# An SSM convolution with gated FFN, forward and backward: the kernel factors are generated over 128x16 positions, kept in DRAM and DMA-transposed for the parameter gradients

## The chip, the cores and the metric

One core of a Trainium2 chip runs the whole program. The metric is the device time of one execution in microseconds. Beside the times there is one execution taken by the hardware profiler; all durations below come from that one.

## The reference, cut to what matters

A diagonal state space model is turned into a convolution kernel, applied to the layer norm of the input, and multiplied by a gated FFN. The program computes the output and the gradients of everything by `jax.vjp`. L is 2048 positions, D 576 channels, N 128 states, F 4608.

```python
def _A_ref(u, A_re, A_im, B_re, B_im, C_re, C_im, log_dt, Dskip):
    dt = jnp.exp(log_dt)[:, None]
    logdA = dt * (A_re + 1j * A_im)
    dB = dt * (B_re + 1j * B_im)
    P = jnp.exp(logdA[:, :, None] * l[None, None, :])      # l = 0 .. L-1
    K = jnp.einsum("dn,dnl,dn->dl", Cc, P, dB).real
    ...                                                    # y = irfft(rfft(u) * rfft(K)), cut to L
    return y + u * Dskip
def _B_ref(x, w1, w3, w2):
    return (silu(x @ w1) * (x @ w3)) @ w2

xn = layernorm(x)
out = x + _A_ref(xn, ...) * silu(_B_ref(xn, w1, w3, w2))
```

The gradients of A, B, C and dt need, for every channel and state, the sum over all positions of the gradient of K times the same powers P.

## The kernel before, in words

A position l is written as l = b + BV * a. The power at l is the product of a factor q(b) and a factor p(a), so that only BV + AV values per channel and state are computed instead of 2048. Before, BV is 64 and AV is 32 (`Cfg.make`). Channels are taken in 36 chunks of 16.

*Start (0 to about 110 us).* `phase2_params` splits the rates into bf16 pieces and stores them in DRAM (`PCS_dram`). `build_selectors` makes two selector matrices, SEL and SELR, of 16 * (BV + AV) columns with GpSimd iotas and VectorE operations; after them comes the layer norm.

*Exp tables (`ssm_early`, about 110 to 200 us).* For each chunk TensorE multiplies the rates with SELR (L381), ScalarE takes Exp (L384) and SyncE's queue stores the table E to DRAM (L385). The Fourier transform of the input runs between these matmuls on TensorE.

*Kernel generation (`ssm_kernel`, `kgen_chunk`, about 212 to 548 us).* Per chunk: TensorE makes the phases from SEL (et_ps, L437); VectorE masks them (m_k, L438); ScalarE computes sine, absolute value and cosine (S_k, m_k, C_k in `trig`, L296 to L300); VectorE multiplies with E into q (L444) and p (L446), p with the output weights into t (L456) and v (L459, L460); TensorE multiplies q with v (kps, L465: 64 matmuls on half the array's columns); ScalarE copies the result into KT (L467). GpSimd reorders the half of p that the backward needs into pz, which is stored to DRAM (`PZ_dram`, L452). The forward FFN (`ffn_hidden`) runs on the same engines at the same time: for each half tile 20 matmuls (L673 to L676), five evictions on ScalarE or four there and one on VectorE (s_t, g_t, u_t) and a product on VectorE (h_t, L683).

*Convolution, the FFN's output, the backward of the convolution (about 548 to 1202 us).* These stages are not touched.

*Parameter sums (`param_sums`, `param_chunk`, about 1202 to 1661 us).* The 128 values b = 0 to 127 of each channel are needed here with the position on the partitions, that is, transposed against the forward's q. The program computes them again: rows of `PCS_dram` are loaded (rt, L81), TensorE spreads them with SELB (L904 for Exp, L919 for the phases), ScalarE takes Exp (E_q, L905), VectorE masks (m_q, L920), ScalarE computes sine, absolute value and cosine (S_q, m_q, C_q), VectorE multiplies into qi and qr (L926). Then come 32 matmuls of 32 columns with the gradients gKK (pT, L932), four VectorE products with pz (pr_q, L936) and two sums (S_all, L938). Chunks go in pairs: Exp and sine need different ScalarE tables, and each pair loads both.

*Final products and the FFN's backward (`phase5_final`, `phase6_...`, 1661 us to the end).* Not touched. They start when the parameter sums are done. Here are the DMA transpositions that exist before the change (`nat_transpose`, L1031, all issued on SyncE's queue): w2T, 128x640, from SBUF, and w1T and w3T, 576x128, from DRAM.

The order of the instructions on each engine is fixed at build time by a scheduler that simulates the program. `self.at(us)` gives it a due time: a kernel generation chunk every 8 us, an FFN tile (two half tiles) every 12 us. An engine works its own list strictly in order; an instruction that has to wait holds up all behind it, DMA issues in its queue among them.

Of the kernel before, what the change touches and what calls it, by code (L numbers as in the profile page):

```python
# [10 lines left out]
ACT = mybir.ActivationFunctionType  # L11
ALU = mybir.AluOpType
# [4 lines left out]
P = 128  # L17
# [5 lines left out]
class Cfg:  # L23
# [12 lines left out]
    AV: int = 32  # L36
    BV: int = 64

    @staticmethod
    def make(L, D, N, F, LS=None):  # L40
# [13 lines left out]
        assert L % 64 == 0  # L54
        c.AV = L // 64
        c.BV = 64
        assert c.AV % 2 == 0 and c.AV <= 64
# [3 lines left out]
class K:  # L61
# [206 lines left out]
    def split_rates(self, tmp):  # L268
# [7 lines left out]
        th64 = tmp.tile([P, DT, N], FP32, name="th64")  # L276
        nc.vector.tensor_scalar(out=t[:], in0=thr[:], scalar1=64.0, scalar2=MAGIC, op0=ALU.mult, op1=ALU.add)
        nc.vector.tensor_scalar(out=t[:], in0=t[:], scalar1=-MAGIC, scalar2=None, op0=ALU.add)
        nc.vector.scalar_tensor_tensor(out=th64[:], in0=thr[:], scalar=64.0, in1=t[:], op0=ALU.mult, op1=ALU.subtract)
        for q, src in enumerate((thr, th64, self.rho)):  # L280
# [22 lines left out]
    def build_selectors(self, selp):  # L303
# [4 lines left out]
        SELR = selp.tile([P, QW + PW], BF16, name="SELR")  # L308
        with self.tc.tile_pool(name="sel_tmp", bufs=1) as st:
# [7 lines left out]
            nc.gpsimd.iota(ii[:, QW:], pattern=[[1, 2], [2, AV // 2], [0, DC]], base=0, channel_multiplier=0)  # L317
# [14 lines left out]
            nc.vector.tensor_scalar(out=rc[:], in0=self.pcol[:], scalar1=112.0, scalar2=96.0, op0=ALU.is_equal,  # L332
# [11 lines left out]
    def ssm_forward(self, T0, TK, TC):  # L344
# [4 lines left out]
        self.PZ_dram = self.dram.tile([P, NCH, 3, 16, LT], BF16, name="PZ_dram")  # L349
        self.S_dram = self.dram.tile([P, LT, D], BF16, name="S_dram")  # L350
# [9 lines left out]
    def ssm_early(self, matp):  # L360
# [9 lines left out]
        with self.tc.tile_pool(name="ex_l", bufs=1) as lp, \  # L370
# [7 lines left out]
            for ch in range(NCH):  # L378
                pe = ps.tile([P, TW], FP32, name="e_ps")
                for o in range(0, TW, 512):  # L380
                    nc.tensor.matmul(pe[:, o:o + 512], lhsT=LR_[0:48, ch, :], rhs=self.SELR[0:48, o:o + 512], start=True,  # L381
                                     stop=True)
# [16 lines left out]
    def ssm_kernel(self, T0, TK, ps, ps1):  # L399
# [7 lines left out]
        assert NCH % GE == 0 and AV == 2 * cfg.LT  # L407
# [18 lines left out]
    def kgen_chunk(self, ch, E, lhs, SEL, mp, sb, sb1, ps, ps1):  # L426
        nc, cfg = self.nc, self.cfg
        AV, BV = cfg.AV, cfg.BV
        AH = AV // 2
# [5 lines left out]
        for o in range(0, TW, 512):  # L435
            pt = ps.tile([P, 512], FP32, name="et_ps")
            nc.tensor.matmul(pt[:], lhsT=lhs, rhs=SEL[:, o:o + 512], start=True, stop=True)  # L437
            nc.vector.tensor_scalar(out=m[:, o:o + 512], in0=pt[:].bitcast(I32), scalar1=(1 << 17) - 1, scalar2=None,  # L438
                                    op0=ALU.bitwise_and)
        S, C = self.trig(sb1, m, 17, TW, "k")  # L440
        q = sb.tile([P, 2, DC, BV], BF16, name="q_k")
        p = sb.tile([P, 2, AV, DC], BF16, name="p_k")
        for k, src in enumerate((C, S)):
            nc.vector.tensor_tensor(out=q[:, k].rearrange("p d b -> p (d b)"), in0=E[:, 0:QW], in1=src[:, 0:QW],  # L444
                                    op=ALU.mult)
            nc.vector.tensor_tensor(out=p[:, k].rearrange("p a d -> p (a d)"), in0=E[:, QW:], in1=src[:, QW:],  # L446
                                    op=ALU.mult)
        pz = sb.tile([P, 3, DC, AH], BF16, name="pz_k")
        ph = p[:, :, 0:AH, :].rearrange("p r a d -> p r d a")
        nc.gpsimd.tensor_copy(out=pz[:, 1:3], in_=ph)  # L450
# [10 lines left out]
        kps = ps1.tile([P, DC, AH], FP32, name="kps")  # L461
        for dl in range(DC):
            for hf in range(2):
                for k in range(2):
                    nc.tensor.matmul(kps[64 * hf:64 * hf + 64, dl, :], lhsT=q[:, k, dl, :],  # L465
                                     rhs=v[:, k, hf * AH:(hf + 1) * AH, dl], start=(k == 0), stop=(k == 1))
# [401 lines left out]
    def param_sums(self, gKK, S_all):  # L868
# [4 lines left out]
        W_ = DC * N  # L873
        GE = 2
        with self.tc.tile_pool(name="g_big", bufs=1) as big, \
                self.tc.tile_pool(name="g_e", bufs=GE + 1) as ep, \
                self.tc.tile_pool(name="g_gen", bufs=2) as gen, \
                self.tc.tile_pool(name="g_t", bufs=2) as tp_, \
                self.tc.tile_pool(name="g_ps0", bufs=3, space=bass.MemoryType.PSUM) as ps0, \
                self.tc.tile_pool(name="g_ps", bufs=2, space=bass.MemoryType.PSUM) as ps:  # L880
            SELB = big.tile([P, P], BF16, name="SELB")
            r0 = big.tile([P, 1], FP32, name="selb_r0")
            nc.vector.tensor_scalar(out=r0[:], in0=self.pcol[:], scalar1=0.0, scalar2=192.0, op0=ALU.is_equal,
                                    op1=ALU.mult)
            r1 = big.tile([P, 1], FP32, name="selb_r1")
            nc.vector.tensor_scalar(out=r1[:], in0=self.pcol[:], scalar1=0.0, scalar2=None, op0=ALU.is_gt)
# [4 lines left out]
            for rt in rts:  # L891
                nc.vector.memset(rt[0:1, :], 1.0)
# [454 lines left out]
```

## Time and profile before

| | us |
|---|---|
| median of 3 runs | 2834.83 |
| the runs | 2826.5 to 2841.63 |
| the profiled execution: time | 2835.69 |
| the profiled execution: span | 2833.8 |
| kernel generation, first m_k to last KT | 212.0 to 547.9 |
| parameter sums, first q_ps to last S_all | 1202.5 to 1661.3 |

Over the whole span PE is busy 75%, DVE 57%, ACT 47% and POOL 14% of the time, and the mean granted TensorE clock is 0.832 of full speed. These averages mix stages with quite different limits; a row that gives the busy time of each engine in one stretch says more. In the profile's rows PE is TensorE, PEld its weight loads, DVE VectorE, ACT ScalarE, POOL GpSimd, SP SyncE; a name with q behind it (SPq, ACTq) is that engine's queue of DMA issues. A group row gives line, engine, operation, out<-in, shapes and count, then the busy time in us and the mean duration in ns, then the idle time of the engine before these instructions and who ended it. A tile row gives the shortest, median and longest duration in ns and the first and last start in us. Neighbouring instructions of an engine overlap by a few tens of ns, so that busy times are somewhat below count times mean.

### The profile page before, as it was taken

What the parts mean: (1) busy time and instruction counts of PE and PEld (TensorE: products, weight loads), DVE (VectorE), ACT (ScalarE), POOL (GpSimd) and SP (SyncE); (2) the same over time, 40 slices, a digit from 0 to 9 for tenths busy, and PEclk for the clock granted to TensorE, in tenths of its full rate; (3) what the DMA queues carried; (4) which work ended last, traced back from release to release, by engine and by line L of the source; (5) the groups of instructions that cost most, each with busy time, mean ns of one, the idle gap of its engine ahead of it and who ended that gap; (6) DMA issues with size and microseconds to landing.
All of it is one profiled execution on the core that took longest, in us unless ns stands there. A gap on an engine that the chain in (4) does not pass through costs nothing. (4 is left out here: it accounts for less than half of the span.)

```text
span 2833.8 us, 42478 instructions
## 1 busy us (share of the span) xinstructions
PE 2127.6 (75%) x17097; PEld 1348.5 (48%) x17190; DVE 1606.1 (57%) x2512; ACT 1319.3 (47%) x1633; POOL 389.1 (14%) x655
## 2 busy tenths in 40 slices
PE   1799899999698545455545416999999999828999
PEld 1233344455476323221222214776777677616777
DVE  7218899888255798967777793444434434202222
ACT  1449899855111302077777725756556556100000
POOL 0003444311210000000000001222222222100000
PEclk9559999999899777755555558999999999969999
DMA  3346566654765132100000027545445443475441
GB/s 73 111 179 223 181 210 213 232 198 155 284 217 156 50 99 69 48 19 19 19 19 16 16 62 185 163 141 141 129 138 151 125 147 111 97 173 201 168 171 66
DMA packets 326297, 366.56 MB, mean 129 GB/s; under 512 B 117242, under 2 KB 276220, under 8 KB 322900
## 3 DMA queue, kind: packets, MB, share of 16 engines
q1 hardware_dynamic: 192844, 160.89, 19.1%
q0 software_dynamic: 34704, 109.15, 11.4%
q10 hardware_dynamic: 98552, 93.80, 10.7%
q8 instruction: 134, 2.20, 0.3%
q14 instruction: 63, 0.52, 0.1%
HBM read 182.55 MB, written 164.42 MB: 122 GB/s over the span
## 5 line engine op out<-in xcount | busy, mean ns | idle before, releaser
L1219 PE MATMUL px<-w1T,ggc 128*128 128x288 bf16 x1152 | 237.9, 289 | 43.5 <-DMA w1T<-in_B_w_dram 43.5
L1219 PE MATMUL px<-w3T,guc 128*128 128x288 bf16 x1152 | 237.7, 288 | 28.9 <-DMA guc<-GU_dram 19.2
L1167 PEld LDWEIGHTS <-xn_bf 128*128 128x128 bf16 x2304 | 225.8, 98 | 57.5 <-issue 29.6
L1126 PE MATMUL ph<-go_oT,w2T 128*128 128x512 bf16 x682 | 162.7, 382 | 48.0 <-DMA go_oT<-GOT_dram 44.4
L1170 DVE CAST gw<-pgw 128x256 bf16<-128x256 f32 x144 | 60.1, 423 | 224.8 <-DMA out_dram<-gw 129.6
L1236 ACT ACTIVATE t<-gx 128x576 f32<-128x576 f32 x16 | 10.9, 683 | 364.5 <-DVE gx L1223 364.5
L1223 DVE TENSOR_TENSOR gx<-px,gx 128x288 f32<-128x288 f32 x32 | 13.1, 452 | 293.3 <-PE px L1219 293.3
L673 PEld LDWEIGHTS <-wmB_w 128*128 128x128 bf16 x1152 | 103.1, 99 | 140.3 <-issue 45.4
L727 PE MATMUL po<-w2g,hc 128*128 128x288 bf16 x1152 | 149.0, 292 | 25.1 <-DMA hc<-H_dram 20.0
L1155 PE MATMUL pgw<-go_o,h_n 128*128 128x288 bf16 x1152 | 164.9, 286 | 0.9
L673 PE MATMUL pg<-xnT,wmB_w 128*128 128x512 bf16 x538 | 156.6, 388 | 10.1 <-DVE g_t L679 7.8
L673 PE MATMUL pu<-xnT,wmB_w 128*128 128x512 bf16 x559 | 158.9, 386 | 1.5 <-issue 0.5
L1167 PE MATMUL pgw<-gg_n,xn_bf 128*128 128x256 bf16 x1152 | 133.5, 276 | 26.2 <-DVE gw L1170 26.2
L1219 PEld LDWEIGHTS <-ggc 128*128 128x128 bf16 x1152 | 113.5, 99 | 73.9 <-issue 44.6
L932 PE MATMUL pT<-gKK,qr 128*128 128x32 bf16 x576 | 69.0, 233 | 97.6 <-DVE qr L926 97.6
L1219 PEld LDWEIGHTS <-guc 128*128 128x128 bf16 x1152 | 113.4, 98 | 59.7 <-DMA guc<-GU_dram 19.8
L727 PEld LDWEIGHTS <-hc 128*128 128x128 bf16 x1152 | 113.5, 100 | 57.1 <-issue 25.9
L1094 POOL DMA_DIRECT2D gate<-G_dram x36 | 19.3, 538 | 877.2 <-PE sT_ps L951 769.2
L1167 PE MATMUL pgw<-gu_n,xn_bf 128*128 128x256 bf16 x1152 | 137.5, 273 | 0.0
L919 PE MATMUL q_ps<-rt,SELB 4*128 4x512 bf16 x144 | 80.0, 580 | 72.4 <-DVE m_q L920 70.3
L1126 PEld LDWEIGHTS <-w2T 128*128 128x128 bf16 x720 | 69.0, 98 | 119.7 <-DMA out_dram<-gl_bf 38.6
L1129 ACT CAST gh<-ph 128x512 bf16<-128x512 f32 x144 | 82.3, 587 | 90.2 <-PE ph L1126 90.2
(337 smaller groups left out, 5106.3 us busy)
## 6 DMA issues: line engine op xcount, KB each, us to landing
G_dram<-g_t POOLq DMA_DIRECT2D x72, 256.0 KB, 2.7
U_dram<-u_t POOLq DMA_DIRECT2D x72, 256.0 KB, 3.5
H_dram<-h_t SPq DMA_DIRECT2D x72, 256.0 KB
hc<-H_dram SPq DMA_DIRECT2D x8, 2304.0 KB
gate<-G_dram POOLq DMA_DIRECT2D x36, 512.0 KB, 4.5
up<-U_dram POOLq DMA_DIRECT2D x36, 512.0 KB, 6.1
GU_dram<-guT ACTq DMA_DIRECT2D x36, 512.0 KB
GG_dram<-ggT ACTq DMA_DIRECT2D x36, 512.0 KB
```

The lines of the kernel that those rows point to most:

```text
L673: nc.tensor.matmul(pt[:], lhsT=wm[w][:, c, cs], rhs=xnT[:, c, t0:t0 + 512], start=(c == 0), stop=False)
L727: nc.tensor.matmul(po_[:, pi_, 0:pw], lhsT=hc[:, fi, k * P:(k + 1) * P], rhs=w2[fi][:, po:po + pw], start=(fi == 0), stop=(fi == FT - 1))
L919: nc.tensor.matmul(pt[:], lhsT=SELB[0:4, :], rhs=rt[0:4, o:o + 512], start=True, stop=True)
L932: nc.tensor.matmul(pT[:, dl, k, :], lhsT=q[:, dl, :], rhs=gKK[:, :, :, d0 + dl], start=True, stop=True)
L1094: nc.gpsimd.dma_start(out=gate[:], in_=self.G_dram[fi])
L1126: nc.tensor.matmul(ph[:, q * 512:(q + 1) * 512], lhsT=w2T[:, c, :], rhs=go_oT[:, c, hh * HL + q * 512:hh * HL + (q + 1) * 512], start=(c = ...
L1129: nc.scalar.copy(out=gh[:, hh * HL:(hh + 1) * HL], in_=ph[:])
L1155: nc.tensor.matmul(pgw[pi_][:, 0:pw], lhsT=h_ns[fl][:, tt, :], rhs=go_o[:, tt, po:po + pw], start=(tt == 0), stop=(tt == LT - 1))
L1167: nc.tensor.matmul(pw_[:, 0:GW], lhsT=self.xn_bf[:, tt, c * P:(c + 1) * P], rhs=nat[:, tt, :], start=(tt == 0), stop=(tt == LT - 1))
L1170: nc.vector.tensor_copy(out=gw[:], in_=pw_[:, 0:GW])
L1219: nc.tensor.matmul(px[pi_][:, 0:pw], lhsT=act[:, fi, k * P:(k + 1) * P], rhs=wT[:, fi, po:po + pw], start=(fi == 0 and ai == 0), stop=(fi ...
L1223: nc.vector.tensor_tensor(out=gx[:, po:po + pw], in0=px[pi_][:, 0:pw], in1=gx[:, po:po + pw], op=ALU.add)
```

## The change

1. BV becomes 128 and AV 16. A chunk has 16 * (128 + 16) = 2304 columns in place of 1536: E tables, selectors, phases, masks and the three ScalarE passes are that wide. q doubles to 2048 columns; p, t and v halve to 256. The kps matmuls become 32 on the full array in place of 64 on half of it. The masks use 16 bits in place of 17.
2. E is made in two pieces (1536 and 768 columns) per chunk. The pools of E and m in the kernel generation have two buffers in place of three. SELR gets a pool of its own that ends before the FFN starts.
3. With 128 positions b, the forward's q is what the backward needs, transposed. The forward stores q to DRAM (`Q_dram`, 1 MB per chunk, 36 chunks), issued from ScalarE's queue.
4. `param_sums` loads it with one DMA transposition per chunk on SyncE's queue (128x4096 into 128x32x128) and pz on ScalarE's queue. Everything that made qi and qr again is gone: the rt loads, SELB, the Exp, the masks, the sines and the products.

```diff
-        c.AV = L // 64
-        c.BV = 64
+        c.AV = L // P
+        c.BV = P
...
             for ch in range(NCH):
-                pe = ps.tile([P, TW], FP32, name="e_ps")
-                for o in range(0, TW, 512):
-                    nc.tensor.matmul(pe[:, o:o + 512], lhsT=LR_[0:48, ch, :], rhs=self.SELR[0:48, o:o + 512], start=True,
-                                     stop=True)
                 E = ep.tile([P, TW], BF16, name="E_k")
-                nc.scalar.activation(out=E[:], in_=pe[:], func=ACT.Exp)
+                for h0 in range(0, TW, 1536):
+                    hw = min(1536, TW - h0)
+                    pe = ps.tile([P, 1536], FP32, name="e_ps")
...
+                    nc.scalar.activation(out=E[:, h0:h0 + hw], in_=pe[:, 0:hw], func=ACT.Exp)
...
-                self.tc.tile_pool(name="kg_e", bufs=3) as ep, \
-                self.tc.tile_pool(name="kg_m", bufs=3) as mp, \
+                self.tc.tile_pool(name="kg_e", bufs=2) as ep, \
+                self.tc.tile_pool(name="kg_m", bufs=2) as mp, \
...
         for k, src in enumerate((C, S)):
+            nc.vector.tensor_tensor(out=p[:, k].rearrange("p a d -> p (a d)"), in0=E[:, QW:], in1=src[:, QW:],
+                                    op=ALU.mult)
+        for k, src in enumerate((C, S)):
             nc.vector.tensor_tensor(out=q[:, k].rearrange("p d b -> p (d b)"), in0=E[:, 0:QW], in1=src[:, 0:QW],
                                     op=ALU.mult)
...
+        nc.scalar.dma_start(out=self.Q_dram[ch], in_=q[:].rearrange("p k d b -> p (k d b)"))
...
         for dl in range(DC):
-            for hf in range(2):
-                for k in range(2):
-                    nc.tensor.matmul(kps[64 * hf:64 * hf + 64, dl, :], lhsT=q[:, k, dl, :],
-                                     rhs=v[:, k, hf * AH:(hf + 1) * AH, dl], start=(k == 0), stop=(k == 1))
+            for k in range(2):
+                nc.tensor.matmul(kps[:, dl, :], lhsT=q[:, k, dl, :], rhs=v[:, k, :, dl], start=(k == 0), stop=(k == 1))
...
+        with self.tc.tile_pool(name="g_q", bufs=3) as qp, \
+                self.tc.tile_pool(name="g_t", bufs=3) as tp_, \
+                self.tc.tile_pool(name="g_ps", bufs=3, space=bass.MemoryType.PSUM) as ps:
+            for ch in range(NCH):
+                d0 = ch * DC
+                qT = qp.tile([P, 2 * DC, N], BF16, name="qT")
+                self.nat_transpose(qT[:], self.Q_dram[ch])
+                pz = tp_.tile([P, 3, DC, LT], BF16, name="pz")
+                nc.scalar.dma_start(out=pz[:], in_=self.PZ_dram[:, ch])
+                pT = ps.tile([P, DC, 2, 2 * LT], FP32, name="pT")
+                for dl in range(DC):
+                    for k in range(2):
+                        nc.tensor.matmul(pT[:, dl, k, :], lhsT=qT[:, (1 - k) * DC + dl, :], rhs=gKK[:, :, :, d0 + dl],
+                                         start=True, stop=True)
...
```

The order changes with it. On ScalarE in the middle of the kernel generation, before, from the cosine of one chunk (C_k_3207) to the copy of the same chunk's result (KT from kps_3226); numbers tell tiles of one name apart:

```order
L300 ACTIVATE C_k_3207<-m_k_3194,halfpi_col_70 128x1536
L677 ACTIVATE s_t_7049<-pg_7051 128x512
L682 CAST u_t_7048<-pu_7052 128x512
L677 ACTIVATE s_t_7049<-pg_7066 128x512
L681 CAST g_t_7047<-pg_7066 128x512
L682 CAST u_t_7048<-pu_7067 128x512
L296 ACTIVATE S_k_3304<-m_k_3294,npi_col_72 128x1536
L677 ACTIVATE s_t_7087<-pg_7089 128x512
L682 CAST u_t_7086<-pu_7090 128x512
L298 ACTIVATE m_k_3294<-m_k_3294,nhalf_col_74 128x1536
L467 CAST KT_1247<-kps_3226 128x16x16
```

The same place after the change, from C_k_2887 past the copy of its own chunk (kps_2907); Q_dram<-q_k_2889 is the issue of that chunk's store:

```order
L298 ACTIVATE C_k_2887<-m_k_2868,halfpi_col_70 128x2304
L678 ACTIVATE s_t_6298<-pg_6315 128x512
L682 CAST g_t_6296<-pg_6315 128x512
L683 CAST u_t_6297<-pu_6316 128x512
L678 ACTIVATE s_t_6336<-pg_6338 128x512
L451 DMA Q_dram_1383<-q_k_2889 128x4096
L468 CAST KT_1396<-kps_2907 128x16x16
L683 CAST u_t_6335<-pu_6339 128x512
L678 ACTIVATE s_t_6336<-pg_6353 128x512
L682 CAST g_t_6334<-pg_6353 128x512
```

Between the cosine and the copy there stood nine instructions, two of them passes of the next chunk; now there are four evictions of the FFN and the store's issue. In four of every six chunks the copy stands right behind the store's issue; in the other two, three or four more evictions stand between.

On SyncE's queue at the end of the parameter sums, before: the last loads of rt and pz, then two transpositions for the FFN's backward, then the stores of the gradients (gout, gl_bf).

```order
L81 DMA rt_12340<-PCS_dram 3x2048
L81 DMA rt_12341<-PCS_dram 3x2048
L81 DMA pz<-PZ_dram 128x768 x3
L1031 DMA_TRANSPOSE w2T<-w2r_15754 128x5x128
L1031 DMA_TRANSPOSE w2T<-w2r_15834 128x5x128
L81 DMA out_dram<-gout 128x128 x12
```

After, from the last load of the convolution's backward (gs):

```order
L850 DMA gs<-GS_dram 128x4x288 x2
L986 DMA_TRANSPOSE qT<-Q_dram 128x32x128 x36
L986 DMA_TRANSPOSE w2T<-w2r_13717 128x5x128
L986 DMA_TRANSPOSE w2T<-w2r_13797 128x5x128
L79 DMA out_dram<-gout 128x128 x12
```

All 36 transpositions stand in one block in place of the rt and pz loads; what follows them is as before.

More of the change, by code (lines that the diff above doesn't have):

```diff
@@ L35 @@
     M: int = 1023
-    AV: int = 32
-    BV: int = 64
+    AV: int = 16
+    BV: int = 128
     @staticmethod
@@ L307, in build_selectors @@
         SEL = selp.tile([P, QW + PW], BF16, name="SEL")
-        SELR = selp.tile([P, QW + PW], BF16, name="SELR")
+        SELR = selrp.tile([P, QW + PW], BF16, name="SELR")
         with self.tc.tile_pool(name="sel_tmp", bufs=1) as st:
@@ L349, in ssm_forward @@
         self.PZ_dram = self.dram.tile([P, NCH, 3, 16, LT], BF16, name="PZ_dram")
+        self.Q_dram = self.dram.tile([NCH, P, 2 * 16 * P], BF16, name="Q_dram")
         self.S_dram = self.dram.tile([P, LT, D], BF16, name="S_dram")
```

122 lines of the change are left out of this document (31 added, 91 removed).

## The prediction

> **What bounds the kernel now.** I read the busy time by stretch first, cutting the span where the tile views put the first and last instruction of each stage. The columns are the stretch, its length, the busy time and count of PE, PEld, DVE, ACT and POOL, then the granted clock, the DMA share and GB/s.
>
> ```profile
> 110.00:200.00 90.00, 88.30 (x257) 26.79 (x256) 14.38 (x19) 52.66 (x37) 0.00 (x0) 0.50 0.46 184
> 228.00:547.00 319.00, 292.41 (x3312) 130.55 (x3349) 286.08 (x480) 284.21 (x377) 141.93 (x170) 0.97 0.63 205
> 1202.00:1662.00 460.00, 230.88 (x1452) 98.86 (x1451) 346.57 (x460) 329.72 (x290) 3.36 (x8) 0.50 0.08 23
> 1662.00:1724.00 62.00, 5.41 (x14) 2.04 (x15) 38.06 (x215) 10.89 (x9) 1.91 (x5) 0.53 0.49 98
> ```
>
> The change touches three of these. From 110 to 200 (the Exp tables) PE is full, at half clock. From 228 to 547 (kernel generation beside the FFN) PE, DVE and ACT are each at about 90%, so whatever is added to one of them can show. From 1202 to 1662 (the parameter sums) no engine is full and DMA idles: a loop of short steps sets the time. The timeline of DVE shows that loop, here from one pair of chunks to the next:
>
> ```profile
> 1400.14 1.89 DVE L936 TENSOR_TENSOR pr_q<-pT,pz 128x512 f32<-128x512 f32 x3 [0.15 <-PE pT L932]
> ...
> 1422.05 1.23 DVE L926 TENSOR_TENSOR qr<-E_q,C_q 128x2048 bf16<-128x2048 bf16 x1 [4.45 <-ACT C_q L300]
> ...
> 1425.33 1.29 DVE L936 TENSOR_TENSOR pr_q<-pT,pz 128x512 f32<-128x512 f32 x2 [0.16 <-PE pT L932]
> ```
>
> One pair takes 1425.33 - 1400.14 = 25.2 us, 12.6 us a chunk; DVE waits on ACT's sines, ACT on DVE's masking. The tile views give the ends of the stage, and the groups what a chunk costs:
>
> ```profile
> L904 PE MATMUL q_ps<-rt,SELB x144: 577/582/630, 1202.5 to 1630.2; 3*128 3x512 bf16 x144
> ```
> ```profile
> L938 DVE TENSOR_REDUCE S_all<-pr_q x72: 1207/1209/1214, 1225.9 to 1660.1; 128x32 f32<-128x1024 f32 x72
> ```
> ```profile
> L936 DVE TENSOR_TENSOR pr_q<-pT,pz 128x512 f32<-128x512 f32 x144 | 92.1, 681 | 2.5 <-PE pT L932 1.3
> L938 DVE TENSOR_REDUCE S_all<-pr_q 128x32 f32<-128x1024 f32 x72 | 87.1, 1209 | 0.0
> L932 PE MATMUL pT<-gKK,qi 128*128 128x32 bf16 x576 | 73.8, 233 | 47.4 <-DVE qi L926 47.4
> L300 ACT ACTIVATE C_q<-m_q,halfpi_col 128x2048 bf16<-128x2048 f32 x36 | 69.8, 1986 | 0.0
> L932 PE MATMUL pT<-gKK,qr 128*128 128x32 bf16 x576 | 69.0, 233 | 97.6 <-DVE qr L926 97.6
> L926 DVE TENSOR_TENSOR qr<-E_q,C_q 128x2048 bf16<-128x2048 bf16 x36 | 44.1, 1225 | 89.3 <-ACT C_q L300 89.3
> ```
>
> The stage runs from 1202.5 to 1661.3: 459 us.
>
> **The backward part: what goes.** All of Exp, masking, sines and the two q products go, and with them every wait on ACT. What stays per chunk is DVE's four products and two sums, 4 x 92.1/144 + 2 x 87.1/72 = 4.98 us, and PE's 32 matmuls, (73.8 + 69.0)/36 = 3.97 us, beside DVE. What is added is one DMA transposition of 1,048,576 bytes per chunk on SP's queue. What is late next is either DVE or that transposition, and the trace has only small ones:
>
> ```profile
> L1031 SPq DMA_TRANSPOSE w2T<-w2r x36: 1200/1202/2217, 1663.6 to 2378.1; - x36
> L1031 SPq DMA_TRANSPOSE w1T<-in_B_w_dram x36: 1165/1264/4421, 2451.1 to 2556.5; - x36
> ```
> ```profile
> L717 SPq DMA_DIRECT2D hc<-H_dram x8: 328/328/798, 730.9 to 849.7; - x8
> ```
> ```profile
> 2473.15 1.26 SPq L1031 DMA_TRANSPOSE w1T<-in_B_w_dram  x1
> 2474.46 1.26 SPq L1031 DMA_TRANSPOSE w3T<-in_B_w_dram  x1
> ```
> ```profile
> q1 hardware_dynamic: 13834, 3.36, 51.7%
> ```
> ```profile
> q10 hardware_dynamic: 2928, 4.08, 3.2%
> ```
>
> A plain load of 2304 KB holds SP for 0.328 us; a transposition of 147,456 bytes (w1T) holds it for 1.264 us, one of 163,840 bytes (w2T) for 1.202. Size does not lengthen a plain issue, so the excess, 0.94 or 0.87 us, belongs to transposing. If it grows with bytes, a chunk's issue is 0.33 + 7.11 x 0.94 = 7.0 us by w1T, or 0.33 + 6.4 x 0.87 = 5.9 us by w2T. If it does not grow, the DMA engines set the pace: from 2470 to 2500, with nothing else moving, 3.36 MB took 51.7% of 30 us, so 1.05 MB takes 4.84 us; the chunk's pz load (ACT's queue moved 4.08 MB in 3.2% of the stage's 460 us) adds 0.7: 5.5 us. If all of it grows, at the pitch of 1.31 us between two starts, it is 7.11 x 1.31 = 9.3 us. I take 6.5 us, between the two readings of the excess. With 12 us to fill and drain (one issue, one landing, one round of DVE) the stage is 36 x 6.5 + 12 = 246 us: **-213 us**. Bounds: 36 x 5.5 + 12 = 210 (-249) and 36 x 9.3 + 12 = 347 (-112). The 62 us behind it (1662 to 1724, DVE's final products) stay: SP has the same two w2T transpositions ahead of the gradient stores as before.
>
> The Trainium skill, in "Advanced Engine Details and Errata", section "X-Bar Transpose (TRN2)", says that transposing DMAs run as fast as plain ones, at 350 to 400 GB/s. By it a chunk's transposition would take about 2.8 us (an estimate from that page), against 4.84 us by the row, and the sum would end at DVE's pace.
>
> **The forward part: what is added.** Width goes from 1536 to 2304 columns per chunk, in three places.
>
> *Kernel generation.* The groups of 228 to 547:
>
> ```profile
> L438 DVE TENSOR_SCALAR m_k<-et_ps 128x512 int32<-128x512 int32 x100 | 64.2, 678 | 5.1 <-PE et_ps L437 4.4
> L677 ACT ACTIVATE s_t<-pg 128x512 bf16<-128x512 f32 x95 | 57.2, 603 | 19.1 <-PE pu L676 18.6 <-PE pg L675 0.3
> L300 ACT ACTIVATE C_k<-m_k,halfpi_col 128x1536 bf16<-128x1536 f32 x35 | 55.8, 1595 | 0.0
> L465 PE MATMUL kps<-v_k,q_k 128*64 128x16 bf16 x2287 | 52.2, 191 | 17.5 <-DVE v_k L459 15.9 <-DVE v_k L460 0.3
> L456 DVE TENSOR_TENSOR t_k<-p_k,nWiT 128x1024 bf16<-128x1024 bf16 x35 | 37.2, 1062 | 0.0
> L437 PE MATMUL et_ps<-SEL,lhs_t 128*128 128x512 bf16 x98 | 30.7, 385 | 1.5 <-DVE m_k L438 1.5
> L683 DVE TENSOR_TENSOR h_t<-s_t,u_t 128x1024 bf16<-128x1024 bf16 x49 | 34.3, 701 | 3.7 <-ACT u_t L682 3.6
> L444 DVE TENSOR_TENSOR q_k<-E_l,C_k 128x1024 bf16<-128x1024 bf16 x35 | 24.0, 685 | 13.8 <-ACT C_k L300 13.8
> L459 DVE TENSOR_TENSOR v_k<-t_k 128x512 bf16<-128x512 bf16 x36 | 16.7, 465 | 0.0
> L446 DVE TENSOR_TENSOR p_k<-E_l,C_k 128x512 bf16<-128x512 bf16 x35 | 14.5, 415 | 0.0
> L467 ACT CAST KT<-kps 128x256 bf16<-128x256 f32 x35 | 13.0, 371 | 7.9 <-PE kps L465 7.7
> ```
> ```profile
> L1136 ACTq DMA_DIRECT2D GU_dram<-guT x36: 366/366/385, 1736.6 to 2418.6; - x36
> ```
>
> ACT: 2048 columns cost 1.986 us and 1536 cost 1.595, so 768 more cost 0.59 us; three passes in 36 chunks are 63 us, and the 36 Q stores issued from ACT's queue, at 0.366 us, 13 more: 284 + 76 = 360 us of work for 319 us. ACT becomes the bound. With no idle time that is +41 us; at today's busy share (284/319 = 0.89) the stage takes 404 us, +85. To this comes a new wait: the KT copy now stands close behind its own cosine. From the end of C_k, DVE does p (0.2), q (1.2), two t (1.0), the FFN's h (0.7) and two v (0.5), then PE its kps matmuls (64 half-wide ones took 64 x 52.2/2287 = 1.46; about 1.4 now), with 0.3 for handing over: 5.3 us. ACT has four 0.60 us instructions and one issue, 2.8 us, to fill them, and behind the waiting KT copy stand the evictions of the FFN that free PE's banks. Before, nine instructions (7.4 us) stood between the two for a chain of 6.5 us, and KT waited 7.7 us in all. At 2.5 us in two chunks of three that adds 61 us (+146); I take a quarter of it, since a late ACT lets DVE and PE run ahead: **+100**.
>
> DVE's own sum barely moves: masking +0.96 and products +1.0 a chunk, t -1.0, v and p -0.8. PE gets 1.5 more et_ps matmuls (0.31 us each, +17 us in all). Both are hidden under ACT's 404 us (286 and 292 busy now). DMA gets 37.7 MB of Q and 7.1 MB of E, by the best stretch at hand
>
> ```profile
> 2560.00:2570.00 10.00, 9.33 (x65) 6.83 (x65) 3.42 (x8) 0.78 (x2) 0.00 (x0) 0.83 0.87 324
> ```
>
> at 324/0.87 = 372 GB/s 120 us beside the present 0.63 x 319 = 201: a share of 0.80 in 404 us, hidden, but without slack if ACT were faster.
>
> *Exp tables and selectors.*
>
> ```profile
> 191.45 1.46 PE L381 MATMUL e_ps<-SELR,lhs_r 48*128 48x512 bf16 x3
> ```
> ```profile
> 30.89 1.03 POOL L313 IOTA ii<- 128x1024 int32 x1 [27.28 <-DMA lhs_t<-PCS_dram]
> ```
> ```profile
> 39.90 0.42 DVE L341 TENSOR_SCALAR SELR<-val 128x512 bf16<-128x512 f32 x1
> ```
>
> PE is full from 110 to 200, so half again as many Exp matmuls show in full: 36 x 1.46/2 = **+26 us**; ACT's wider Exp fits beside it (52.7 of 90 us busy). The selectors, on the path to the layer norm, take 9.4 us now, half again later: **+5**.
>
> Sum: -213 + 100 + 26 + 5 = -82 us on the profiled execution's 2835.7 us, which is within 1 us of the median of the runs shown: **2754 us**.
>
> **The rivals.**
> *The transposition keeps up.* If SP's issue does not grow with size, the DMA engines' 5.5 us set the pace: 2835.7 - 249 + 131 = 2718 us; if the engines were faster still, DVE's 4.98 us: 36 x 4.98 + 12 = 191, 2699 us. That is what the skill's rule of the section named above would make of it. For it: plain issues show no growth. Against: in the small transpositions SP, not the engines, was the one that was full.
> *ACT waits for every KT copy.* 85 + 36 x 2.5 = 175: 2835.7 - 213 + 175 + 31 = 2829 us, no change. For it: the new order. Against: the 7.7 us of today.
> *SP pays for every byte.* At 9.3 us a chunk the backward gain is 112 us and the forward cost 131: 2855 us, slower. It decides at (459 - 131 - 12)/36 = 8.8 us a chunk. For it: w2T and w1T, nearly one size, cost nearly the same, which leaves proportion open. Against: a fixed part of 0.33 us is there in every plain issue.
>
> **How the numbers follow.** Chances: forecast 0.50, transposition keeps up 0.27, ACT waits 0.10, SP pays 0.13. The forecast's own range is -235 + 72 to -195 + 177, 2673 to 2818 us (5.9 to 7.0 us a chunk, generation +41 to +146). The range of 8 in 10, 2670 to 2850, adds the bulk of the first two rivals and leaves out most of the last and the best corner. One half per cent, 14 us, is about what a measurement of this kernel can tell from none. Faster by more: the first two nearly whole, some of the third: 0.80; within: 0.08; slower: 0.12.
>
> **What would show it.** Right: qT transpositions back to back on SP, 6 to 7 us apart, DVE waiting on them; ACT over 90% busy in generation, about 400 us long; Exp tables 26 us longer. Wrong: qT starts 5 us apart or 9; generation still near 320 us (then PE or DVE had hidden slack) or above 470.

## The result, and the profile after

The changed kernel takes 2758.5 us (median of 4 runs, 2757.1 to 2761.6), the kernel before 2833.7 (4 runs, 2826.5 to 2841.6): a ratio of 0.9736, 95% interval 0.9708 to 0.9763. The profiled execution took 2761.6 us with a span of 2759.7. The forecast was 2754 us. The total came out, but by luck: two of its terms erred by about 60 us each, in opposite directions.

The stretches of the changed kernel, in the columns of the prediction's first fence: Exp tables, kernel generation, parameter sums.

```profile
113.00:245.00 132.00, 118.76 (x360) 44.90 (x359) 17.42 (x23) 78.10 (x74) 0.00 (x0) 0.50 0.48 193
245.00:744.00 499.00, 379.53 (x2309) 150.07 (x2346) 342.12 (x567) 364.70 (x392) 163.82 (x174) 0.80 0.65 228
1396.00:1583.00 187.00, 74.73 (x1164) 67.83 (x1163) 168.44 (x217) 1.17 (x2) 3.36 (x8) 0.50 1.11 236
```

The generation has no full engine any more: ACT is busy 364.70 of 499 us (73%), PE 76%, DVE 69%, and the granted clock fell from 0.97 to 0.80. In the parameter sums it is the other way round: ACT is empty, and the DMA engines are full (share 1.11). The tile views give the ends of the stages (ns shortest, median and longest, first and last start in us):

```profile
L386 ACT ACTIVATE E_k<-e_ps x72: 805/1128/1452, 113.5 to 244.1; 128x1536 bf16<-128x1536 f32 x36, 128x768 bf16<-128x768 f32 x36
L440 DVE TENSOR_SCALAR m_k<-et_ps x180: 406/675/693, 245.5 to 717.1; 128x512 int32<-128x512 int32 x144, 128x256 int32<-128x256 int32 x36
L468 ACT CAST KT<-kps x36: 372/372/405, 265.7 to 743.8; 128x256 bf16<-128x256 f32 x36
L858 ACTq DMA_DIRECT2D GXN_dram<-gx x32: 326/326/395, 1219.7 to 1396.0; - x32
L986 SPq DMA_TRANSPOSE qT<-Q_dram x36: 4536/5334/6671, 1381.1 to 1567.2; - x36
L893 DVE TENSOR_REDUCE S_all<-pr_q x72: 1208/1210/1215, 1402.8 to 1581.9; 128x32 f32<-128x1024 f32 x72
```

From these and the same views of before, cut at the first Exp, the first m_k, the end of the last KT, the last store of the convolution's gradient and the end of the last sum (us):

| stretch | before | after | difference | forecast |
|---|---|---|---|---|
| start, selectors | 110.0 | 113.5 | +3.5 | +5 |
| Exp tables, to the first m_k | 102.0 | 132.0 | +30 | +26 |
| kernel generation | 335.9 | 498.7 | **+163** | +100 |
| convolution, FFN output, backward of the convolution | 654.6 | 651.8 | -3 | 0 |
| parameter sums | 458.8 | 187.1 | **-272** | -213 |
| the rest | 1172.5 | 1176.6 | +4 | 0 |
| span | 2833.8 | 2759.7 | -74 | -82 |

*The generation.* ACT's waits in it (us in total, times, longest):

```profile
ACT KT L468 <- PE kps L467: 69.4, 19, 5.8
ACT s_t L678 <- PE pg L676: 41.2, 15, 5.0
ACT KT L468 <- DVE m_k L440: 18.1, 6, 3.0
...
ACT s_t L678 <- PE pu L677: 2.5, 3, 1.0
```

and PE's on ACT's evictions (copies of finished matmul results out of PE's accumulation banks, which PE needs free again), from 262 to 744:

```profile
PE pg L674 <- ACT g_t L682: 23.1, 22, 2.7
PE pu L674 <- ACT u_t L683: 22.8, 6, 3.8
```

ACT stands at KT copies for 69.4 + 18.1 = 87.5 us, where it stood 7.7 before. One such wait, in ACT's timeline (start, us, engine, line, what; the idle time before it in brackets):

```profile
474.67 2.23 ACT L298 ACTIVATE C_k<-m_k,halfpi_col 128x2304 bf16<-128x2304 f32 x1
476.78 0.60 ACT L678 ACTIVATE s_t<-pg 128x512 bf16<-128x512 f32 x1
477.26 0.60 ACT L682 CAST g_t<-pg 128x512 bf16<-128x512 f32 x1
...
478.20 0.64 ACT L678 ACTIVATE s_t<-pg 128x512 bf16<-128x512 f32 x1
478.39 0.34 ACTq L451 DMA_DIRECT2D Q_dram<-q_k  x1
482.66 0.37 ACT L468 CAST KT<-kps 128x256 bf16<-128x256 f32 x1 [3.81 <-PE kps L467]
```

The same stretch of DVE, the chain that the KT copy waits for:

```profile
476.93 0.29 DVE L446 TENSOR_TENSOR p_k<-E_l,C_k 128x256 bf16<-128x256 bf16 x1 [2.63 <-ACT C_k L298]
477.14 1.22 DVE L449 TENSOR_TENSOR q_k<-E_l,C_k 128x2048 bf16<-128x2048 bf16 x1
478.27 1.33 DVE L459 TENSOR_TENSOR t_k<-p_k,WrT 128x512 bf16<-128x512 bf16 x1
479.53 0.61 DVE L459 TENSOR_TENSOR t_k<-p_k,nWiT 128x512 bf16<-128x512 bf16 x1
480.06 0.68 DVE L684 TENSOR_TENSOR h_t<-s_t,u_t 128x1024 bf16<-128x1024 bf16 x1
480.67 0.28 DVE L462 TENSOR_TENSOR v_k<-t_k 128x256 bf16<-128x256 bf16 x1
...
```

And PE, at its end:

```profile
481.44 1.18 PE L467 MATMUL kps<-v_k,q_k 128*128 128x16 bf16 x31
```

C_k ends at 476.90, the KT copy can start at 482.66: a chain of 5.8 us (the prediction had 5.3). ACT has four evictions to put into it, at a pitch of 477.26 - 476.78 = 0.48 us: 1.9 us. The 0.60 us that a row shows is the duration of an instruction whose successor has already started, so that durations overstate the cover. The next sine, 2.2 us of work that needs none of this, stands behind the KT copy.

*The parameter sums.* The groups of 1396 to 1583 (busy us, mean ns, idle time before them and who ended it), then the queues' packets, MB and share of the 16 DMA engines:

```profile
L891 DVE TENSOR_TENSOR pr_q<-pT,pz 128x512 f32<-128x512 f32 x144 | 93.2, 681 | 18.6 <-PE pT L886 13.6 <-DMA pz<-PZ_dram 5.0
L886 PE MATMUL pT<-gKK,qT 128*128 128x32 bf16 x1152 | 71.5, 234 | 112.1 <-DMA qT<-Q_dram 108.5 <-DVE gx L857 3.6
```
```profile
q1 hardware_dynamic: 139261, 35.38, 96.0%
q10 hardware_dynamic: 5328, 7.23, 12.6%
```

Transpositions start (1567.2 - 1381.1)/35 = 5.32 us apart. PE waits for them 108.5 us, DVE only 18.6 in all.

### The profile page after: what moved, and what is told of

Read it like the earlier page. It is cut to its first block, busy times and chain, and to the rows that moved or that the text cites. A ratio compares the mean times of both kernels' runs of the same rounds, so it can differ in the third digit from the quotient of the medians.

```text
span 2759.7 us, 39491 instructions
## 1 busy us (share of the span) xinstructions
PE 2061.2 (75%) x15803; PEld 1342.9 (49%) x15894; DVE 1473.6 (53%) x2361; ACT 1083.3 (39%) x1381; POOL 409.0 (15%) x655
## 3 DMA queue, kind: packets, MB, share of 16 engines
q10 hardware_dynamic: 106112, 134.65, 14.6%
## 4 chain that ended last, share of the span: by engine, by line
PE 24%; DMA 11%; DVE 10%; issue 7%; SPq 4%; POOL 3%; ACT 0%; POOLq 0%; DVEq 0%; ACTq 0%
PE px L1174 10%; DMA qT<-Q_dram 5%; PE ph L1081 5%; SPq L986 4%; DMA out_dram<-gw 3%; PE pgw L1122 3%; PE pgw L1110 2%; PE ptr L994 1%; DVE cm_t L564 1%; DMA w2T<-w2r 1%; PE et_ps L525 1%; DVE Z L562 1%; DVE cm_t L561 1%; POOL out_dram L1126 1%; DVE Z L565 1%
## 5 line engine op out<-in xcount | busy, mean ns | idle before, releaser
L674 PEld LDWEIGHTS <-wmB_w 128*128 128x128 bf16 x1152 | 110.1, 103 | 213.7 <-issue 130.6
L674 PE MATMUL pg<-xnT,wmB_w 128*128 128x512 bf16 x535 | 162.2, 405 | 42.1 <-ACT g_t L682 24.0
L674 PE MATMUL pu<-xnT,wmB_w 128*128 128x512 bf16 x565 | 170.0, 415 | 24.8 <-ACT u_t L683 24.4
L886 PE MATMUL pT<-gKK,qT 128*128 128x32 bf16 x1152 | 71.5, 234 | 112.1 <-DMA qT<-Q_dram 108.5
L1174 PEld LDWEIGHTS <-guc 128*128 128x128 bf16 x1152 | 113.7, 99 | 60.2 <-DMA guc<-GU_dram 19.5
L453 POOL COPY pz_k<-p_k 128x512 bf16<-128x512 bf16 x36 | 73.2, 2035 | 433.6 <-DVE p_k L446 433.6
L440 DVE TENSOR_SCALAR m_k<-et_ps 128x512 int32<-128x512 int32 (+1 forms) x180 | 103.4, 625 | 56.3 <-PE et_ps L439 56.3
L1110 PEld LDWEIGHTS <-h_n 128*128 128x128 bf16 x1152 | 108.8, 98 | 31.2 <-issue 1.0
```

The costliest lines, as they stand in the source:

```text
L440: nc.vector.tensor_scalar(out=m[:, o:o + ow], in0=pt[:, 0:ow].bitcast(I32), scalar1=(1 << 16) - 1, scalar2=None, op0=ALU.bitwise_and)
L453: nc.gpsimd.tensor_copy(out=pz[:, 1:3], in_=p[:].rearrange("p r a d -> p r d a"))
L674: nc.tensor.matmul(pt[:], lhsT=wm[w][:, c, cs], rhs=xnT[:, c, t0:t0 + 512], start=(c == 0), stop=False)
L886: nc.tensor.matmul(pT[:, dl, k, :], lhsT=qT[:, (1 - k) * DC + dl, :], rhs=gKK[:, :, :, d0 + dl], start=True, stop=True)
L1110: nc.tensor.matmul(pgw[pi_][:, 0:pw], lhsT=h_ns[fl][:, tt, :], rhs=go_o[:, tt, po:po + pw], start=(tt == 0), stop=(tt == LT - 1))
L1174: nc.tensor.matmul(px[pi_][:, 0:pw], lhsT=act[:, fi, k * P:(k + 1) * P], rhs=wT[:, fi, po:po + pw], start=(fi == 0 and ai == 0), stop=(fi ...
```

## The experiments

The kernels that leave out the Q stores, the pz copies or loads, or half of DVE's products, or that load Q plainly, do not compute all parameter gradients. The theory for the generation: ACT, working in order, stands at KT copies and evictions that wait for a chain from the cosine through DVE and PE, because the order leaves too little independent work between. Rivals: two m_k buffers in place of three; the bytes of Q; the Q issue on ACT itself; simply too much work for ACT. For the parameter sums: the transposition sets the pace, either by the DMA engines or by SP's issue. All times are medians of 4 runs with a ratio to the kernel before on the same chip, or a single profiled run where no ratio is given.

### The KT copy due later

```diff
+        self.tc.cur_priority += 8000
         nc.scalar.copy(out=self.KT[:, :, d0:d0 + DC], in_=kps[:].rearrange("p d a -> p a d"))
```

> The changed kernel with one edit: the KT copy is given a due time 8 us later, so that in ACT's order it stands behind the next chunk's sine (four short evictions, the Q issue, two more and the 2.2 us sine between a cosine and its KT copy, instead of four or five short instructions). Nothing else is moved on purpose. Theory (ACT, working in order, stands at KT copies for 87.5 of the 482 us of the generation, and the evictions behind them starve PE): the waits at KT fall below 25 us and the generation from 499 to 425-445 us, so 2690 to 2710 us. Rival, two m_k buffers: at most 10 us gained. Rival, the traffic of the Q stores: nothing gained. Rival, ACT simply has too much work: nothing gained.

Measured: 2724.4 us, ratio 0.9624 (0.9592 to 0.9656), generation 245.4 to 705.0 = 460 us. Its stretch and ACT's waits in it:

```profile
245.00:705.00 460.00, 360.48 (x2349) 146.60 (x2348) 337.36 (x567) 366.11 (x395) 170.45 (x174) 0.87 0.71 249
```
```profile
ACT s_t L679 <- PE pu L678: 72.2, 25, 4.1
ACT KT L469 <- PE kps L467: 7.2, 6, 1.3
```

ACT's work is the same (366 us against 365), so too much work is not what made 499 us. The waits at the KT copy are gone as expected, but only 39 of the 54 to 74 us came back: ACT now waits at evictions of the FFN. In PE's timeline, 12 of these 25 waits, 37 of 72 us, have kps matmuls of the chain ahead of the matmuls waited for. There the wait has moved to another instruction behind the chain, and the theory has to speak of all that stands behind kps, not of the KT copy alone. In the other half PE is at FFN matmuls that come late for other reasons (in this stage it waits 50.4 us for masks, m_k, and 32.7 us for g_t on DVE); what sets those was not tested.

### The Q stores on SP's queue

```diff
-        nc.scalar.dma_start(out=self.Q_dram[ch], in_=q[:].rearrange("p k d b -> p (k d b)"))
+        nc.sync.dma_start(out=self.Q_dram[ch], in_=q[:].rearrange("p k d b -> p (k d b)"))
```

> The changed kernel with the Q stores issued from SP's queue instead of ACT's: the same bytes, but ACT has 36 issues fewer, and its order comes out as before the change, with the KT copy behind the next sine in most chunks. Theory (waits at the KT copy): most of the 87.5 us goes, generation 430 to 460 us, 2700 to 2730 us. Rival, the traffic of the Q stores: unchanged, 2750 to 2765 us, or slower, since SP's loads of E_l stand behind stores that wait for q_k. Rival, two m_k buffers: unchanged.

Measured: **2667.9 us**, ratio 0.9418 (0.9391 to 0.9446), 91 us faster than the changed kernel; generation 245.7 to 646.6 = 401 us. The stretch, the wait that is largest in it on ACT, and one chunk of ACT's timeline:

```profile
245.00:647.00 402.00, 349.30 (x2346) 143.47 (x2346) 338.98 (x567) 367.84 (x394) 164.77 (x174) 0.90 0.79 282
```
```profile
ACT KT L468 <- PE kps L467: 15.9, 23, 2.7
```
```profile
463.61 2.21 ACT L298 ACTIVATE C_k<-m_k,halfpi_col 128x2304 bf16<-128x2304 f32 x1
...
468.91 2.22 ACT L294 ACTIVATE S_k<-m_k,npi_col 128x2304 bf16<-128x2304 int32 x1
471.39 0.37 ACT L468 CAST KT<-kps 128x256 bf16<-128x256 f32 x1 [0.27 <-PE kps L467]
```

The next sine now stands ahead of the KT copy (in 33 of 36 chunks; in the changed kernel in 5) and fills the chain. ACT's work is again 368 us, its idle time 402 - 368 = 34 us in place of 134, its share 0.915. The gain is larger than expected: this is the generation that the prediction described (ACT over 90% busy, about 400 us).

### No Q stores

```diff
-        nc.scalar.dma_start(out=self.Q_dram[ch], ...)
+        if ch == 0:
+            nc.scalar.dma_start(out=self.Q_dram[ch], ...)
...
-                self.nat_transpose(qT[:], self.Q_dram[ch])
+                self.nat_transpose(qT[:], self.Q_dram[0])
```

> The changed kernel with 35 of the 36 Q stores left out; the parameter sums then load the first chunk's Q 36 times (the parameter gradients are left out in that sense). ACT's order is that of the run with the stores on SP's queue. Theory (waits at the KT copy): within 10 us of that run, since the bytes fit beside the work. Rival, the traffic of the Q stores: 40 us or more faster than that run, and E_l's landing back from 6.8 us to under 5.

Measured: 2661.9 us, ratio 0.9401 (0.9373 to 0.9428).

```profile
245.00:648.00 403.00, 353.42 (x2345) 143.84 (x2344) 339.24 (x567) 367.68 (x395) 162.66 (x174) 0.89 0.61 193
```

The generation is as long as with the stores on SP's queue (402 us), though the DMA share falls from 0.79 to 0.61. The 36 MB are hidden, as forecast; traffic is out as a cause.

### Three m_k buffers

```diff
-                self.tc.tile_pool(name="kg_m", bufs=2) as mp, \
+                self.tc.tile_pool(name="kg_m", bufs=3) as mp, \
+                self.tc.tile_pool(name="kg_sc", bufs=1) as sc, \
...
-        S, C = self.trig(sb1, m, 16, TW, "k")
+        S, C = self.trig(sc, m, 16, TW, "k")
```

> The changed kernel with three m_k buffers again, paid for with one buffer each instead of two for the sine and cosine tiles S_k and C_k; ACT's order stays that of the changed kernel. Theory (waits at the KT copy): within 10 us of the changed kernel, 2750 to 2770 us. Rival, two m_k buffers (masking waits until a cosine has read its tile, PE behind it): 40 us or more faster, 2720 us or less.

Measured: 2760.7 us, ratio 0.9747 (0.972 to 0.9774): no difference from the changed kernel. The waits at the KT copy are the same too:

```profile
ACT KT L469 <- PE kps L468: 68.5, 19, 5.0
```

The smaller pool is out. (That the single S_k and C_k buffers took back what a third m_k gave is not excluded by this run alone, but with two m_k buffers the run with the stores on SP's queue has 34 us of idle time left in all.)

### The Q stores later, on ACT's queue

```diff
+        self.tc.cur_priority += 8000
         nc.scalar.dma_start(out=self.Q_dram[ch], in_=q[:].rearrange("p k d b -> p (k d b)"))
+        self.tc.cur_priority -= 8000
```

> The changed kernel with the Q stores still on ACT's queue, but with a due time 8 us later, so that in ACT's order they stand behind the next chunk's cosine or close to it, and the KT copies behind the next sine in most chunks, as before the change. Same bytes, same queue. Theory (what costs is where the Q issue and the KT copy stand in ACT's order, not the issue and not the bytes): generation 400 to 435 us instead of 499, 2665 to 2705 us. Rival (a store of 1 MB issued from ACT's queue is what costs, wherever it stands): generation 480 to 500 us, 2740 to 2760 us.

Measured: 2732.9 us, ratio 0.9653 (0.9631 to 0.9674), generation 469 us. Neither theory's range held it.

```profile
ACT KT L470 <- PE kps L469: 56.8, 23, 4.6
ACT s_t L680 <- PE pu L679: 18.1, 21, 2.0
```

A store on ACT's queue does not cost the whole 499 - 401 = 98 us wherever it stands: 30 came back by moving it. But the order did not become that of the run with SP's queue. Counting ACT's list from each cosine to its KT copy (an eviction as 0.48 us, a pass of sine or cosine as 2.12, the pitch between starts), the mean work between them, beside ACT's idle time in the generation (length less busy time):

| kernel | work between cosine and KT copy, us | ACT idle, us |
|---|---|---|
| changed kernel | 2.6 | 499 - 365 = 134 |
| Q later, on ACT | 4.0 | 470 - 367 = 103 |
| KT copy later | 7.4 | 460 - 366 = 94 |
| Q on SP's queue | 5.1 | 402 - 368 = 34 |

Take a chain of 5.8 us and add up what each chunk's work leaves of it uncovered: 114 us for the changed kernel, 65 for Q later and 25 for Q on SP's queue, of 134, 103 and 34 us idle. By this count the order accounts for most of the idle time in the first and the last, and for two thirds in Q later; what the other 38 us there are, and whether the store costs ACT something of its own, stays open. The KT copy due later is the exception: there the evictions wait, as above. What in the scheduler's simulation puts the sine behind the KT copy when the store is on ACT's list was not tried.

### The chain made shorter: no pz copies

```diff
-        pz = sb.tile([P, 3, DC, AV], BF16, name="pz_k")
-        nc.gpsimd.tensor_copy(out=pz[:, 1:3], in_=p[:].rearrange("p r a d -> p r d a"))
+        if ch == 0:
+            pz = sb.tile([P, 3, DC, AV], BF16, name="pz_k")
+            nc.gpsimd.tensor_copy(out=pz[:, 1:3], in_=p[:].rearrange("p r a d -> p r d a"))
...
```

> The changed kernel with the pz copies on POOL and their stores left out for 35 of 36 chunks; the parameter sums load the first chunk's pz 36 times. ACT keeps its work and, but for one chunk in six, its order. In the changed kernel the first of the two t_k products takes 1.33 us and the second, of the same size, 0.61; the first runs beside POOL's pz copy. Theory (ACT waits for the chain from the cosine through DVE and PE to the KT copy): without the copy the first takes 0.6 us too, the chain is 0.7 us shorter in every chunk, and the generation 36 x 0.7 = 25 us shorter: 2730 to 2742 us. Rival (ACT's work or its Q issues set the time): within 8 us of the changed kernel.

Measured: 2738.8 us, ratio 0.9676 (0.966 to 0.9692), generation 481 us, 18 less. The two t_k products of the changed kernel, then of this one (ns):

```profile
L459 DVE TENSOR_TENSOR t_k<-p_k,WrT x36: 1324/1332/1341, 261.3 to 739.4; 128x512 bf16<-128x512 bf16 x36
L459 DVE TENSOR_TENSOR t_k<-p_k,nWiT x36: 609/610/614, 262.6 to 740.7; 128x512 bf16<-128x512 bf16 x36
```
```profile
L460 DVE TENSOR_TENSOR t_k<-p_k,WrT x36: 415/419/1333, 261.2 to 721.0; 128x512 bf16<-128x512 bf16 x36
L460 DVE TENSOR_TENSOR t_k<-p_k,nWiT x36: 415/418/609, 262.4 to 721.3; 128x512 bf16<-128x512 bf16 x36
```

The chain is shorter by 1.33 + 0.61 - 2 x 0.42 = 1.1 us, more than the 0.7 expected, and the time is inside the theory's range, though the stage gave back 18 us and not 25. In ACT's and PE's timelines the time from the end of a cosine to the end of its chunk's kps falls by 1.0 us in the median chunk (5.7 to 4.8) but by 0.57 on average (6.1 to 5.5): 36 x 0.57 = 20 us, about what the stage gave back. ACT has the same work (365 us) and the same number of issues and, but for one chunk in six, the same order, so a shorter chain makes the stage shorter: ACT waits for it.

### Half of DVE's products; then Q by a plain load; then two queues

```diff
-                for s in range(2):
+                for s in range(1):
```
```diff
-                self.nat_transpose(qT[:], self.Q_dram[ch])
+                nc.sync.dma_start(out=qT[:].rearrange("p a n -> p (a n)"), in_=self.Q_dram[ch])
```
```diff
-                self.nat_transpose(qT[:], self.Q_dram[ch])
+                (nc.sync if ch % 2 == 0 else nc.scalar).dma_start_transpose(out=qT[:], in_=self.Q_dram[ch])
```

> The changed kernel with one of the two halves of the products and sums of each chunk left out (two of the four parameter sums are zero), so that DVE has 2.3 to 2.5 us a chunk instead of 4.6 to 5.0. From the last store of the convolution's gradient to the last sum the changed kernel takes 187 us. Theory (the transposition sets the pace): 180 to 190 us, and PE waits longer on qT. Rival (DVE sets it): PE's weight loads are next, 36 x 4.0 + 12 = 156 us or less.

> As the run with half of DVE's products, and Q loaded by a plain DMA instead of a transposing one: the same 1 MB a chunk, on the same queue, in the wrong layout. If transposing DMAs run as fast as plain ones, the stage is as long as in that run (180 to 190 us). If transposing is what slows the DMA engines, PE's weight loads are next: 140 to 160 us.

> As the run with half of DVE's products, with every second transposition issued from ACT's queue instead of SP's. Theory (the DMA engines set the pace): no change against that run, within 4 us. Rival (SP's issue of 5.3 us a transposition sets it, as the prediction's main case had it): two queues share it, and the stage falls to PE's 140 to 160 us.

The stretch of the parameter sums and the loads, for half of DVE's products:

```profile
1395.00:1578.00 183.00, 73.69 (x1160) 67.28 (x1159) 89.93 (x109) 1.08 (x2) 1.79 (x4) 0.50 1.15 234
```

with the plain load:

```profile
1394.00:1508.00 114.00, 73.73 (x1162) 67.76 (x1162) 90.18 (x112) 1.17 (x2) 2.24 (x6) 0.51 0.94 370
```
```profile
L881 SPq DMA_DIRECT2D qT<-Q_dram x36: 319/320/433, 1379.8 to 1494.7; - x36
```

With two queues the stage takes 240 us (1403 to 1643).

With half of DVE's work (89.93 us in place of 168.44) the stage is 4 us shorter: DVE does not set it, the transposition does. The same bytes loaded plainly come (1494.7 - 1379.8)/35 = 3.28 us apart, so transposing is what costs. The stage fell further than expected, to 114 us: PE needs only 74 us, not the 143 that durations of overlapping matmuls had given. Two queues are 57 us slower, which neither theory had. In that run pz stood behind transpositions on ACT's queue, so the next pair of runs leaves pz out.

### One pz for all chunks, on one queue and on two

```diff
-                pz = tp_.tile([P, 3, DC, LT], BF16, name="pz")
-                nc.scalar.dma_start(out=pz[:], in_=self.PZ_dram[:, ch])
+                if ch == 0:
+                    pz = tp_.tile([P, 3, DC, LT], BF16, name="pz")
+                    nc.scalar.dma_start(out=pz[:], in_=self.PZ_dram[:, 0])
```

> As the run with half of DVE's products, with pz loaded for the first chunk alone and used in all. Theory (the DMA engines set the pace and pz takes its share of them): the stage of 183 us falls by 36 x 0.5 to 0.7 us, to 157 to 167 us, 4.5 to 4.8 us a chunk. Rival (SP's issue sets it): within 5 us of 183.

> As the run before it, with every second transposition issued from ACT's queue; no pz loads stand behind them there any more. If the DMA engines set the pace: as the run before it, within 5 us. If one queue's issue sets it: down to PE's 145 to 155 us. If two queues of transpositions hinder one another, as their 240 us with the pz loads leave open: 200 us or more.

The transpositions on one queue, and the stretch:

```profile
L988 SPq DMA_TRANSPOSE qT<-Q_dram x36: 4438/4776/5646, 1380.5 to 1556.3; - x36
```
```profile
1396.00:1568.00 172.00, 73.17 (x1153) 66.82 (x1151) 90.14 (x110) 1.17 (x2) 2.08 (x4) 0.50 1.03 209
```

and on two, with the last line of that view, the time from issue to landing:

```profile
L881 SPq DMA_TRANSPOSE qT<-Q_dram x18: 4411/4559/5906, 1379.5 to 1615.9; - x18
L881 ACTq DMA_TRANSPOSE qT<-Q_dram x18: 4429/4570/4853, 1386.4 to 1622.9; - x18
...
DMA to landing us min/median/max: 6.5/6.7/7.8
```

On one queue the pitch falls from 5.32 to (1556.3 - 1380.5)/35 = 5.02 us and the stage to 172: 11 us, between the 18 to 25 of the DMA engines and the 0 of SP. On two queues it rises to (1622.9 - 1379.5)/35 = 6.95 us, about the 6.7 that one takes to land: a transposition on one queue starts when that on the other has landed. The instruction list shows why: with two queues each transposition is preceded by a wait for the semaphore that the one before it, on the other queue, sets when it has landed. So these runs cannot say whether SP or the DMA engines set the 5.02 us. The engines' share of 1.03 speaks for the engines, and so does their time for one transposition, 1.03 x 5.02 = 5.2 us on one queue and, with the share of 0.76 of the two-queue run (1402 to 1635), 0.76 x 6.95 = 5.3 us with one in flight at a time. That an issue takes 4.57 us even then says that SP is close behind. This stays open.

### The cosine's chain split

Starting from the Q stores on SP's queue:

```diff
-        for t, W in ((t1, self.WrT), (t2, self.nWiT)):
-            nc.vector.tensor_tensor(out=t[:].rearrange("p r a d -> p (r a) d"), ...
+        for r in (1, 0):
+            for t, W in ((t1, self.WrT), (t2, self.nWiT)):
+                nc.vector.tensor_tensor(out=t[:, r], in0=p[:, r], in1=W[:, None, d0:d0 + DC].to_broadcast([P, AV, DC]),
+                                        op=ALU.mult)
```

> The kernel with the Q stores on SP's queue, and the two t_k products split by real and imaginary part, so that the half that needs only the sine is done before the cosine comes: the chain from the cosine to the KT copy is about 1 us shorter. Theory (what idle time is left on ACT, 34 us, is the rest of that wait): 10 to 25 us faster than the 2668 us of the run it starts from. Rival (ACT's work now sets the time): within 8 us of it.

Measured: 2663.6 us, ratio 0.941 (0.9396 to 0.9424): no measurable difference from the kernel that it starts from.

The generation runs from 245.8 to 646.4 = 401 us, as before, and ACT is busy 366 of the 402 us from 245 to 647: its idle time is 36 us, against 34. The time is what the rival said. But this run does not isolate the chain: it became shorter (from the end of the cosine to the end of kps, 6.0 to 5.2 us on average), and the order changed with it, so that the work between cosine and KT copy fell from 5.1 to 4.8 us. The waits at KT fell from 15.9 to 11.6 us and those at the evictions s_t and u_t rose from 14.6 to 19.5. That a shorter chain brings nothing once the order covers it was not shown.

## Why the prediction was right in its total and wrong in two terms

**Parameter sums: right that the transposition sets the pace, wrong in its price.** Forecast -213, measured -272. The gain lies beyond even the bound of -249 that the prediction gave with its sum. The step that failed: "I take 6.5 us, between the two readings of the excess". A transposition started every 5.32 us, within 4% of the 5.5 us that the prediction had worked out for the DMA engines; SP's issue does grow with size (1.26 to 4.6 us for 7 times the bytes), but by less than the excess. That is 36 x 1.18 = 42 us. The other 16 us are the "12 us to fill and drain": the first transposition was issued at 1381.1, 15 us before the convolution's last store at 1396.0, so that filling lay beside other work. DVE waiting on qT, as the forecast said, was PE waiting on it; DVE was nearly the bound itself.

The rule of the Trainium skill that the prediction weighed ("Advanced Engine Details and Errata", section "X-Bar Transpose (TRN2)": transposing DMAs as fast as plain ones, 350 to 400 GB/s) does not hold here: 1.05 MB a chunk came every 5.02 us, 209 GB/s, against 1.25 MB in 3.28 us, 380 GB/s, for the plain load with pz. The same section says that transpositions of two queues must not be in flight together. No run here shows what would happen: the program's own waits keep them apart, at 6.95 us against 5.02.

**Kernel generation: the wait was named, and priced at a sixth.** Forecast +100, measured +163, beyond the prediction's own bound of +146. The work alone was right: with the Q stores elsewhere the generation is 401 us, where the forecast had 404 at today's busy share. The step that failed is "I take a quarter of it, since a late ACT lets DVE and PE run ahead". 15 us were taken for waits, and the order with Q on ACT costs 499 - 401 = 98, or 2.7 a chunk. A late ACT does not let PE run ahead: behind the waiting KT copy stand the evictions that free PE's banks, as the prediction itself says, and PE falls back too: it waits 23.1 + 22.8 us for evictions, and its granted clock is 0.80 for 0.97. Nor was it only the KT copy: of 134 us of idle time, 87.5 stand at KT and 43.7 at s_t. The rival "ACT waits for every KT copy" (0.10) had the right mechanism with 2.5 us a chunk; the wait shown above is 3.8 us, because the chain was 5.8 us (the two t_k products alone took 1.94 us in place of 1.0, beside POOL's copies) and the four evictions and the issue cover 1.9 and not 2.8. "Generation above 470" was named as what would make the prediction wrong, and it came.

**Exp tables and selectors: nearly right.** +30 and +3.5 for +26 and +5. The stage of the Exp tables itself grew by 42 us, from 89 to 131, and 12 us of that were taken back from the gap before the first m_k. ACT's Exp does not quite fit beside PE: PE is busy 119 of 132 us and waits for an Exp 13 times, 11.6 us in all.

**Buffers and bytes, costed at nothing: right.** Two m_k buffers: no difference. (The two E buffers were not tested.) 36 MB of Q: 6 us, within the scatter.

So the likeliest case did not happen as told. The sums came out at the first rival's pace, though it stays open whether the DMA engines set it, and the generation went like the second. The -82 came out near -74 because +63 and -59 cancelled: that is luck.

## What to carry to other kernels

When a change adds a DMA issue or a dependent copy to an engine that works in order, count the independent work between the start of the chain and the first instruction, on any engine, that stands behind its end, by the pitch between starts and not by durations. A wait there is not made good elsewhere if the engine that waits also frees the buffers of the others. And a store that nobody soon waits for is better tried on a queue whose engine has little else to do: here the same bytes from SP's queue were worth 91 us, since ACT's order came out better without them.

## What the runs showed of the hardware that was not expected

*A POOL copy holds up DVE.* The same t_k product takes 1.33 us beside POOL's pz copy, 0.61 beside its second instruction and 0.42 without POOL, and the POOL copy of 512 elements takes 2.04 us:

```profile
477.29 2.04 POOL L453 COPY pz_k<-p_k 128x512 bf16<-128x512 bf16 x1 [4.66 <-DVE p_k L446]
```

It starts while q_k runs (477.14 to 478.36) and ends at 479.33, and the t_k that started at 478.27 ends 0.27 us later. The Trainium skill, in "SBUF — State Buffer", section "Who interferes with whom", has it that VectorE and GpSimd share a port pair as an exclusive lock, so that the later one stands still for the whole instruction; a VectorE instruction with two inputs in SBUF contends with a GpSimd one that reads it. The trace agrees: POOL's copy waits out q_k, and t_k waits out POOL's copy. In the kernel before, a pz copy of the same size that starts beside a DVE instruction reading matmul results (g_t at 316.72 us) takes 1.10 us.

*A transposing DMA of 1 MB costs more than a plain one on both sides:* SP's issue is 4.6 to 5.3 us in place of 0.32, and the DMA engines move 209 GB/s at a share of 1.03 in place of 370 GB/s at 0.94.
